# Weight conversions of the next expert issued within the first expert's second product

## The chip, the cores and the metric

The kernel runs on one core of a Trainium2 chip. The metric is the device time of one execution in microseconds (us). TensorE (PE) multiplies matrices, ScalarE (ACT) and VectorE (DVE) work element by element, GpSimd (POOL) issues the gathers and scatters by index and does some element work, and SyncE (SP) issues the other transfers. The engines run at the same time, each through its own queue of instructions in a fixed order, and wait for each other by semaphores.

## The reference

Attention in which a query sees only the keys of its own cluster, and behind it a mixture of 16 experts (4 groups of 4), where each token goes to one expert:

```python
scores = scale * np.matmul(q, k.transpose(0, 1, 3, 2))
scores = np.where(mask, scores, -1000000000.0)
...
attn = attn / (np.sum(attn, axis=-1, keepdims=True) + 1e-09)
return np.matmul(attn, v).astype(np.float32)
...
        h = np.maximum(xg[mask_e] @ w1[g, e], 0.0)
        ye = h @ w2[g, e]
        combined = g_w[mask_g][mask_e] * e_w[mask_e]
        tok_idx = np.where(mask_g)[0][mask_e]
        out[tok_idx] = combined[:, None] * ye
```

There are 4 x 768 = 3072 tokens of 512 numbers; `w1` of an expert is 512 x 1024, `w2` is 1024 x 512, all float32. The change touches the experts alone.

## The kernel before

**Two parts.** To about 404 us the kernel does the attention and the routing; from there to the end it works through the experts. Tokens are sorted to experts on the chip, each expert has a number of places for tokens (288 for the largest, then fewer), and what doesn't fit is done by a loop at the end, which isn't entered with these inputs.

**Precision.** Each float32 matrix is split into a high and a low float16 part, and a product is made of three matmuls (high x high, high x low, low x high). So each piece of weights has to be converted: `split_chunk` (L948) has ACT write the high part (L952, tile `wh0a` and so on) and DVE the low one (L955, `wl0a`) from a landed piece of float32 weights (`st`). From the 13th piece on POOL does every second high part. Activations are split in the same way: `hh` (ACT, L1172) and `hl` (DVE, L1173) from the bank `psh` of the first product, `yh` (ACT, L1195) and `yl` (DVE, L1196) from the bank `psy` of the second. There are three banks for `psh`, two for `psy` and three for `psm`, which transposes and the last step use.

**The stream of weights.** Weights come in pieces (chunks) of 512 KB: 128 partitions x 1024 float32, four for `w1` and four for `w2` of an expert. `stream` (L1093) is a generator: each step has SP issue the load of a chunk (L945) six ahead of the one that it then converts. A load waits until one of the six buffers for `st` is free, which is when DVE has made the low part of an earlier chunk. Before the loads of an expert's first chunk SP reads the number of that expert into a register (L992, an instruction `TENSOR_LOAD` of the tile `ei`, with two small ones behind it). Tiles with `0` are of `w1`, with `1` of `w2`; `a` and `b` alternate from expert to expert, so the first chunks of the stream go into `wh0a`, then into `wh0b` and `wh1b`.

**The first expert and the group of 128.** The expert with most tokens goes first (`part_a`); its weights were converted during the attention. It has 288 tokens: `up` (L1157) makes eight groups of twelve matmuls (L1170), then `down` (L1176) makes four tiles of 24 matmuls (L1192), each in a bank `psy` that is emptied by `yh` and `yl`. Here the result has features on the partitions; `settle` (L1218) later transposes it back by matmuls with `back` (L1228, three tiles of eight matmuls into `psm`), ACT scales it (`y`, L1234), and POOL scatters it to the output (L1235).

Behind it comes a group of 128 tokens of the same expert (those over 288), the pass with `k = -1` of `ranks` (L1398). Its tokens were transposed at the step `SLT = 13` of the first expert's loop. In this pass PE does eight groups of twelve matmuls of 128 columns (tile `xT`, `wh`, `wl` into `psh`); its second product (L1206) is spread over the next pass, as is each expert's. Then come the expert of rank 0 (288 tokens, weights `wh0a` and `wl0a`), rank 1, and so on.

**What sets the order.** The order of each engine's queue is that of the Python calls, save where `issue_after` puts an instruction behind a named one. In pass -1, at each `i` of the eight groups that is in `FILL` (all eight), one step of `stream` is taken, with its instructions put behind the last gather issued (`self.got`) and behind the eviction `yev[1 + i // 2]` of the first expert. At `i = 5` the tokens of the next expert are transposed (L1142, L1140) and copied to `xT` (L1143): thirds one and three by ACT, the middle one by DVE. At `i = 6` `settle` is called. In the later passes a step of the stream is put behind the last `hl` (`self.ev`). Gathers of tokens (L1127) run on POOL: six in a row for the group of 128 and the first two experts' tokens before the first expert's second product is done, three more while the tokens are transposed.

Of the kernel before, what the change touches and what calls it, by code (L numbers as in the profile page):

```python
# [15 lines left out]
AF = mybir.ActivationFunctionType  # L16
# [870 lines left out]
class Experts:  # L887
# [6 lines left out]
    short = ()  # L894
    AHEAD = 6
    SLT = 13
    FILL, SETTLE, TOK = (0, 1, 2, 3, 4, 5, 6, 7), 2, 5
    HI = (0, 1, 0, 1, 0, 1, 0, 1)
    LEAD = 12
# [257 lines left out]
    def up(self, xT, M, W, h):  # L1157
        nc, R = self.nc, self.R
        KD, FC = R.KD, self.F // P
        w1h, w1l = W  # L1160
        hh = self.xp.tile([P, FC, M], F16, name="hh")
        hl = self.xp.tile([P, FC, M], F16, name="hl")
        h += [hh, hl]
        for f in range(FC):
            fs = slice(f * P, (f + 1) * P)
            ph = next(self.ps_h).tile([P, 512], F32, name="psh")
            i = 0
            for k in range(KD):
                for w, a in ((w1h, 0), (w1h, 1), (w1l, 0)):
                    self.mm = nc.tensor.matmul(out=ph[:, 0:M], lhsT=w[:, k, fs], rhs=xT[:, a, k], start=i == 0, stop=i == 3 * KD - 1)  # L1170
                    i += 1
            nc.scalar.activation(out=hh[:, f], in_=ph[:, 0:M], func=AF.Relu)  # L1172
            self.ev = nc.vector.scalar_tensor_tensor(out=hl[:, f], in0=ph[:, 0:M], scalar=0.0, in1=hh[:, f], op0=ALU.max, op1=ALU.subtract)  # L1173
            yield

# [222 lines left out]
    def ranks(self, bg):  # L1398

        E, sizes = self.R.E, self.sizes  # L1400
        xT, xgs, down = self.xTB, self.xg0, iter(())
        for k in range(-1, E - 1):
            M = self.caps[k] if k >= 0 else P
            if 0 <= k < E - 2:
                xgs = self.gathers(k + 1)
            h = []
            up = self.up(xT, M, self.weights_of(k, 0) if k >= 0 else self.WA[0:2], h)
            for i in range(8):
                while k >= 0 and self.ready < 4 * k + (4 if i >= 4 else 2) or k > 0 and self.ready2 < 4 * k - 4 + (4 if i >= 4 or not self.feature_major(self.caps[k - 1]) else 2):
                    next(self.fill)  # L1410
                next(up, None)
                next(down, None)
                if i == (self.SETTLE if k >= 0 else 6):
                    if k == E - 2:
                        self.tc.keep_in_program_order(self.nc.gpsimd.drain())
                    self.settle()
                if i in self.FILL:
                    with ExitStack() as order:
                        for op in (self.got, self.yev[min(1 + i // 2, 3)]) if k < 0 else (self.ev,):
                            order.enter_context(self.tc.issue_after(op.ins))  # L1420
                        next(self.fill, None)
                if i == self.TOK and k + 1 < E - 1:
                    with self.tc.issue_after(self.mm.ins):
                        nT = self.tokens(xgs, self.caps[k + 1], k < 0)
                if k > 1 and i == 3:
                    with self.tc.issue_after(self.ev.ins):
                        next(bg, None)
            for s in (up, down):
                for _ in s:
                    pass  # L1430
            xT = nT
            if k >= 0:
                cols = [(self.gates[0:m, t, k:k + 1], self.ids[0:m, t, k:k + 1]) for t, m in enumerate(sizes[k])]
                down = self.down(h, M, self.weights_of(k, 1), [g for g, _ in cols], [i for _, i in cols])
            else:
                down = self.down(h, M, self.W2, [self.gB], [self.idB])
        for _ in self.fill:
            pass
        for i, _ in enumerate(down):
            if i == 0:  # L1440
                self.settle()
        self.settle()
        for _ in bg:
            pass
# [102 lines left out]
def tile_cluster_attention_moe(ctx, tc, qT, kT, vr, cen, wr, w1, w2, out):  # L1547
    nc = tc.nc
# [20 lines left out]
    X = Experts(ctx, tc, R, w1, w2, out, stage, wa)  # L1569
# [15 lines left out]
    for i, _ in enumerate(ga):  # L1585
        with tc.issue_after(X.mm.ins):
            if i == X.SLT:
                X.xTB = X.tokens([X.xB], P)

    def late():  # L1590
        yield from X.lists()
        yield from fix.detect()
        fix.finish()
        yield
# [32 lines left out]
```

## Time and profile before

| | |
|---|---|
| median of 3 runs | 744.16 us |
| lowest and highest | 742.54 and 745.04 us |
| the profiled execution, its own time | 743.51 us |
| its span in the trace | 741.8 us |
| PE busy in the span | 717.7 us (97%) |
| DVE busy | 603.6 us (81%) |
| POOL busy | 495.0 us (67%) |
| ACT busy | 481.0 us (65%) |

Times in the trace count from the start of the span. The profile names engine, source line and operation, with the tile that is written and the tiles that are read; an entry `[1.71 <-DVE yl L1196]` behind an instruction says that its engine was idle for 1.71 us before it and what ended that. An instruction's duration overlaps that of its successor by the depth of the pipeline, so the distance from one start to the next is what an instruction costs in a row of such.

### The profile page before, as it was taken

How to read it: one execution, taken by the hardware profiler on the slowest of the kernel's cores; microseconds unless marked ns; L12 is line 12 of the kernel's file. 1: busy time of each engine (PE TensorE's matmuls, PEld its weight loads, DVE VectorE, ACT ScalarE, POOL GpSimd, SP SyncE). 2: the span in 40 equal slices, each digit the busy share in tenths (PEclk: the TensorE clock that was granted, in tenths of full speed). 3: DMA queues.
4: the chain of work that ended last, by engine and by line, in shares of the span. 5: the costliest groups of instructions: out<-in, count | busy, mean ns of one | idle time of the engine just before them, and what ended most of it. 6: DMA issues, size and time to landing. Idle time of an engine off the chain costs nothing.

```text
span 741.8 us, 26652 instructions
## 1 busy us (share of the span) xinstructions
PE 717.7 (97%) x11068; PEld 618.8 (83%) x11068; DVE 603.6 (81%) x1221; ACT 481.0 (65%) x941; POOL 495.0 (67%) x493
## 2 busy tenths in 40 slices
PE   5999999999999999999999989999999999999996
PEld 3688888888888888888888777888789999999996
DVE  7798978799788997989876476767779889999971
ACT  4669877788768887677877176444545455565642
POOL 8899787787787877878787325454744668545632
PEclk9999999999999999999999999999999999999998
DMA  8745734535245351340520696877777688888921
GB/s 259 183 108 163 218 97 117 163 99 152 58 129 176 93 155 45 77 131 2 172 88 24 228 312 216 271 225 223 236 244 234 221 276 270 291 274 267 295 75 35
DMA packets 78616, 128.03 MB, mean 173 GB/s; under 512 B 7667, under 2 KB 45427, under 8 KB 78488
## 3 DMA queue, kind: packets, MB, share of 16 engines
q1 hardware_dynamic: 73404, 112.63, 50.2%
q0 software_dynamic: 4928, 13.59, 5.1%
q8 instruction: 88, 1.44, 0.8%
q14 instruction: 40, 0.33, 0.1%
q10 hardware_dynamic: 156, 0.03, 0.0%
HBM read 93.41 MB, written 13.65 MB: 144 GB/s over the span
## 4 chain that ended last, share of the span: by engine, by line
PE 64%; DVE 17%; issue 6%; ACT 5%; DMA 4%; POOL 2%; POOLq 0%; SPq 0%; DVEq 0%; ACTq 0%
PE psh L1170 14%; PE psy L1192 11%; PE pso L386 6%; PE pso L387 6%; PE psf L360 6%; PE psf L361 6%; DVE mpart L321 5%; PE psc L318 5%; PE psy L1206 3%; DMA B<-parts 2%; PE psm L699 1%; DVE parts L213 1%; ACT p L365 1%; DMA st<-w 1%; PE psm L1228 1%
## 5 line engine op out<-in xcount | busy, mean ns | idle before, releaser
L367 POOL TENSOR_TENSOR pl<-p 128x512 f16<-128x512 f32 x278 | 285.1, 1041 | 72.5 <-ACT p L365 67.9
L321 DVE TENSOR_REDUCE mpart<-psc 128x1 f32<-128x512 f32 (+1 forms) x282 | 190.5, 684 | 29.0 <-PE psc L318 28.5
L365 ACT ACTIVATE p<-psf 128x512 f32<-128x512 f32 x288 | 170.1, 597 | 49.6 <-PE psf L361 44.3
L386 PE MATMUL pso<-V,p 128*128 128x65 f16 x1152 | 160.3, 193 | 0.0
L387 PE MATMUL pso<-V,pl 128*128 128x64 f16 x1152 | 160.0, 193 | 0.0
L386 PE MATMUL pso<-V,pl 128*128 128x65 f16 x1152 | 159.5, 193 | 0.0
L387 PE MATMUL pso<-V,p 128*128 128x64 f16 x1152 | 159.3, 193 | 0.0
L360 PE MATMUL psf<-A 82*128 82x384 f16 (+2 forms) x576 | 144.1, 275 | 1.0 <-ACT p L365 0.9
L361 PE MATMUL psf<-B 128*128 128x384 f16 (+2 forms) x576 | 144.2, 275 | 0.0
L387 PEld LDWEIGHTS <-p 128*128 128x128 bf16 x1152 | 112.3, 97 | 22.1 <-issue 0.2
L386 PEld LDWEIGHTS <-p 128*128 128x128 bf16 x1152 | 113.2, 98 | 9.2 <-issue 1.1
L386 PEld LDWEIGHTS <-pl 128*128 128x128 f16 x1152 | 112.7, 98 | 0.2
L387 PEld LDWEIGHTS <-pl 128*128 128x128 f16 x1152 | 111.5, 97 | 0.1
L318 PE MATMUL psc<-A 80*128 80x512 f16 (+1 forms) x376 | 108.5, 332 | 0.8 <-DVE mpart L321 0.4
L1173 DVE SCALAR_TENSOR_TENSOR hl<-psh,hh 128x160 f16<-128x160 f32 (+14 forms) x136 | 49.7, 368 | 45.6 <-ACT hh L1172 36.6
L1172 ACT ACTIVATE hh<-psh 128x160 f16<-128x160 f32 (+14 forms) x136 | 45.6, 345 | 58.0 <-PE psh L1170 54.9
L1235 POOL DMA_INDIRECT out_dram<-y,ri x33 | 42.0, 1272 | 50.7 <-ACT y L1234 45.3
L1170 PE MATMUL psh<-xT,wh0a 128*128 128x288 f16 (+7 forms) x512 | 74.6, 255 | 0.0
L1127 POOL DMA_INDIRECT xg<-xbuf,ri x25 | 38.6, 1543 | 41.7 <-PE psm L1142 27.9
L361 PEld LDWEIGHTS <-B 128*128 128x128 f16 x576 | 56.9, 99 | 10.6 <-issue 2.0
L1170 PE MATMUL psh<-xT,wh0b 128*128 128x272 f16 (+6 forms) x448 | 64.7, 253 | 0.0
L360 PEld LDWEIGHTS <-A 82*128 82x128 f16 x576 | 56.2, 99 | 10.0 <-issue 1.8
(370 smaller groups left out, 1792.7 us busy)
## 6 DMA issues: line engine op xcount, KB each, us to landing
st<-w SPq DMA_DIRECT2D x128, 512.0 KB
B<-parts SPq DMA_DIRECT2D x64, 192.0 KB
kx<-kT SPq DMA_DIRECT2D x16, 384.0 KB
qx<-qT SPq DMA_DIRECT2D x16, 384.0 KB
vx<-vr SPq DMA_DIRECT2D x16, 384.0 KB
A<-parts SPq DMA_DIRECT2D x32, 192.0 KB
xbuf<-xs SPq DMA_DIRECT2D x4, 1536.0 KB
A<-mk SPq DMA_DIRECT2D x56, 24.0 KB
```

Source lines behind the costliest of these rows:

```text
L318: last["mm"] = nc.tensor.matmul(out=pc[:, off:off + k1 - k0], lhsT=QA[h % 8][0:80, c * P:(c + 1) * P], rhs=KA[h % 8][0:80, k0:k1], start=T ...
L321: nc.vector.tensor_reduce(out=(mp[:, 0, 0:1], mp[:, :, 1], mp[:, 1, 0:1])[i], in_=pc.rearrange("p (a x) -> p a x", a=n), axis=AX.X, op=ALU ...
L360: nc.tensor.matmul(out=o, lhsT=KA[h % 8][0:82, ks], rhs=QA[h % 8][0:82, q0:q1], start=True, stop=False)
L361: nc.tensor.matmul(out=o, lhsT=KBs[h][:, ks], rhs=QBs[h][:, q0:q1], start=False, stop=True)
L365: cfg["exp"] = nc.scalar.activation(out=p32, in_=pf, func=AF.Exp, scale=QK / (SQ * SQ))
L367: lo = (nc.vector if u in (EARLY if h < 2 else DVE_LO[h % 8] if h < NH - 2 else DVE_END) else nc.gpsimd).tensor_tensor(out=pl, in0=p32, in ...
L386: nc.tensor.matmul(out=O[:, col:col + 65], lhsT=p[:, bs], rhs=vh, start=c == 0 and q == 0 and i == 0, stop=False, skip_group_check=True)
L387: nc.tensor.matmul(out=O[:, col:col + 64], lhsT=p[:, bs], rhs=vl, start=False, stop=c == NCH - 1 and i == 1, skip_group_check=True)
L1170: self.mm = nc.tensor.matmul(out=ph[:, 0:M], lhsT=w[:, k, fs], rhs=xT[:, a, k], start=i == 0, stop=i == 3 * KD - 1)
L1172: nc.scalar.activation(out=hh[:, f], in_=ph[:, 0:M], func=AF.Relu)
L1173: self.ev = nc.vector.scalar_tensor_tensor(out=hl[:, f], in0=ph[:, 0:M], scalar=0.0, in1=hh[:, f], op0=ALU.max, op1=ALU.subtract)
L1192: self.mm = nc.tensor.matmul(out=py[:, 0:M], lhsT=w[:, f, d * P:(d + 1) * P], rhs=a[:, f], start=i == 0, stop=i == len(prods) - 1)
```

## The change

Steps of the stream are now also taken in the loop over the first expert's own steps: at steps 10, 12, 14 and 15 of 16 (`SOON`), put behind the last `hl`, the last gather and the last `yh`. In pass -1 only `i` = 1, 3, 5 and 7 take a step (`FILL0`), put behind the last gather and the last `hh` (`self.act`, new). The later passes are as before. Line numbers of the changed kernel are higher by one from L897 on, and by up to six at the end.

```diff
     SLT = 13
+    SOON, FILL0 = (10, 12, 14, 15), (1, 3, 5, 7)
     FILL, SETTLE, TOK = (0, 1, 2, 3, 4, 5, 6, 7), 2, 5
...
-            nc.scalar.activation(out=hh[:, f], in_=ph[:, 0:M], func=AF.Relu)
+            self.act = nc.scalar.activation(out=hh[:, f], in_=ph[:, 0:M], func=AF.Relu)
...
-                if i in self.FILL:
+                if i in (self.FILL if k >= 0 else self.FILL0):
                     with ExitStack() as order:
-                        for op in (self.got, self.yev[min(1 + i // 2, 3)]) if k < 0 else (self.ev,):
+                        for op in (self.got, self.act) if k < 0 else (self.ev,):
                             order.enter_context(self.tc.issue_after(op.ins))
                         next(self.fill, None)
...
             if i == X.SLT:
                 X.xTB = X.tokens([X.xB], P)
+        if i in X.SOON:
+            with ExitStack() as order:
+                for op in (X.ev, X.got) + tuple(X.yev[-1:]):
+                    order.enter_context(tc.issue_after(op.ins))
+                next(X.fill)
```

ACT's queue in the kernel before, from the first expert's first eviction `yh` to the middle of the group of 128 (`hh` of 128 x 128 belongs to that group, `wh0a`, `wh0b` and `wh1b` are converted chunks):

```order
L1195 ACTIVATE yh<-psy 128x288 x2
L952 ACTIVATE wh0a<-st 128x2x512 x2
L1195 ACTIVATE yh<-psy 128x288
L952 ACTIVATE wh0a<-st 128x2x512 x2
L1195 ACTIVATE yh<-psy 128x288
L952 ACTIVATE wh0b<-st 128x2x512
L1172 ACTIVATE hh<-psh 128x128
L952 ACTIVATE wh0b<-st 128x2x512
L1172 ACTIVATE hh<-psh 128x128 x2
L952 ACTIVATE wh1b<-st 128x4x256 x2
L1172 ACTIVATE hh<-psh 128x128 x2
L952 ACTIVATE wh0b<-st 128x2x512
```

The same stretch of ACT's queue in the changed kernel:

```order
L1196 ACTIVATE yh<-psy 128x288
L953 ACTIVATE wh0a<-st 128x2x512
L1196 ACTIVATE yh<-psy 128x288
...
L953 ACTIVATE wh0a<-st 128x2x512 x2
L1196 ACTIVATE yh<-psy 128x288
L1173 ACTIVATE hh<-psh 128x128 x2
L953 ACTIVATE wh0b<-st 128x2x512
...
L1173 ACTIVATE hh<-psh 128x128
L953 ACTIVATE wh1b<-st 128x4x256
L1144 COPY xT<-psm 128x8x128
```

The first two conversions stand each behind an eviction of their own, and in the group of 128 all four conversions into `wh0b` (left out: three more pairs of one `hh` and one `wh0b`) stand ahead of the first into `wh1b`.

DVE's queue in the kernel before, from the last `yl` of the first expert to the copy of the next tokens:

```order
L1196 SCALAR_TENSOR_TENSOR yl<-psy,yh 128x288
L955 SCALAR_TENSOR_TENSOR wl0b<-st,wh0b 128x2x512
L1173 SCALAR_TENSOR_TENSOR hl<-psh,hh 128x128 x3
L955 SCALAR_TENSOR_TENSOR wl0b<-st,wh0b 128x2x512
L955 SCALAR_TENSOR_TENSOR wl1b<-st,wh1b 128x4x256
L1173 SCALAR_TENSOR_TENSOR hl<-psh,hh 128x128 x2
L955 SCALAR_TENSOR_TENSOR wl1b<-st,wh1b 128x4x256
L1173 SCALAR_TENSOR_TENSOR hl<-psh,hh 128x128
L1143 COPY xT<-psm 128x8x128
```

And in the changed kernel:

```order
L1197 SCALAR_TENSOR_TENSOR yl<-psy,yh 128x288
L1174 SCALAR_TENSOR_TENSOR hl<-psh,hh 128x128 x2
L956 SCALAR_TENSOR_TENSOR wl0b<-st,wh0b 128x2x512
L1174 SCALAR_TENSOR_TENSOR hl<-psh,hh 128x128 x2
L956 SCALAR_TENSOR_TENSOR wl0b<-st,wh0b 128x2x512
L1174 SCALAR_TENSOR_TENSOR hl<-psh,hh 128x128 x2
L1144 COPY xT<-psm 128x8x128
L956 SCALAR_TENSOR_TENSOR wl1b<-st,wh1b 128x4x256
```

Two low parts instead of four stand ahead of the copy, and they stand between pairs of `hl`.

SP's queue in the kernel before, where the sixth load of the stream has been issued (`TENSOR_LOAD` of `ei` reads an expert's number; five more follow at once, and only then the seventh load):

```order
L945 ISA
L945 DMA st_11820<-w1 128x2x512
L992 TENSOR_LOAD ei_11487
L992 ISA x2
L992 TENSOR_LOAD ei_11487
```

And in the changed kernel at the same place:

```order
L946 ISA
L946 DMA st_11724<-w1 128x2x512
L946 ISA
L946 DMA st_11755<-w2 128x4x256
L993 TENSOR_LOAD ei_11487
```

The seventh load, which waits for the first free buffer, stands ahead of the register loads. On PE three matmuls of L1206 stand one group of L1170 later, and the first tile of `settle` takes the bank that DVE's copy frees, the second and third those that ACT's copies free. POOL's queue is unchanged.

## Rows read from the trace of the kernel before

**Rows 1.** Waits of PE, 404:742 (waited for: us in total, times, longest us).

```profile
PE psy L1192 <- DVE yl L1196: 2.1, 2, 1.7
PE psh L1170 <- issue: 0.9, 2, 0.5
```

**Rows 2.** Waits of PE, 444.5:742, all of them.

```profile
PE psy L1192 <- DVE yl L1196: 0.4, 1, 0.4
```

**Rows 3.** Timeline of PE, 421:445 (start us, us, instruction xcount [idle before <-releaser]).

```profile
421.77 1.14 PE L1192 MATMUL psy<-hl,wh1a 128*128 128x288 f16 x8
...
427.57 1.14 PE L1192 MATMUL psy<-hh,wh1a 128*128 128x288 f16 x8 [1.71 <-DVE yl L1196]
...
435.90 0.38 PE L1206 MATMUL psy<-wh1a,hh 128*128 128x512 f16 x1
436.12 0.38 PE L1206 MATMUL psy<-wl1a,hh 128*128 128x512 f16 x1
436.96 0.27 PE L1170 MATMUL psh<-xT,wh 128*128 128x128 f16 x2 [0.46 <-DVE hl L1173]
...
438.97 1.06 PE L1142 MATMUL psm<-ident,xg 128*128 128x128 f16 x16
...
440.07 0.27 PE L1170 MATMUL psh<-xT,wh 128*128 128x128 f16 x2
...
441.19 0.22 PE L1228 MATMUL psm<-back,yh 128*128 128x128 f16 x1 [0.30 <-ACT xT L1143]
...
442.53 0.28 PE L1170 MATMUL psh<-xT,wh 128*128 128x128 f16 x2
...
444.42 0.41 PE L1170 MATMUL psh<-xT,wh0a 128*128 128x288 f16 x2
```

**Rows 4.** Timeline of ACT, 419:458.

```profile
426.62 0.71 ACT L1195 ACTIVATE yh<-psy 128x288 f16<-128x288 f32 x2 [6.19 <-PE psy L1192]
...
434.10 0.41 ACT L1195 ACTIVATE yh<-psy 128x288 f16<-128x288 f32 x1 [1.08 <-PE psy L1192]
...
438.98 1.09 ACT L952 ACTIVATE wh0b<-st 128x1024 f16<-128x1024 f32 x1
439.93 0.31 ACT L1172 ACTIVATE hh<-psh 128x128 f16<-128x128 f32 x1
440.09 1.06 ACT L1143 COPY xT<-psm 128x1024 f16<-128x1024 f16 x1
...
444.13 0.28 ACT L1172 ACTIVATE hh<-psh 128x128 f16<-128x128 f32 x1 [1.75 <-PE psm L1228]
...
453.97 1.06 ACT L952 ACTIVATE wh1a<-st 128x1024 f16<-128x1024 f32 x1 [2.38 <-DMA st<-w]
```

**Rows 5.** Timeline of DVE, 419:446.

```profile
427.06 0.82 DVE L1196 SCALAR_TENSOR_TENSOR yl<-psy,yh 128x288 f16<-128x288 f32 x2 [6.15 <-ACT yh L1195]
...
432.12 2.35 DVE L955 SCALAR_TENSOR_TENSOR wl0a<-st,wh0a 128x1024 f16<-128x1024 f32 x2
...
441.23 0.68 DVE L1143 COPY xT<-psm 128x1024 f16<-128x1024 f16 x1
```

**Rows 6.** Timeline of POOL, 414:446: the last gather of each of the two rows.

```profile
424.08 0.95 POOL L1127 DMA_INDIRECT xg<-xbuf,ri  x1 [0.30 <-issue]
...
442.26 0.97 POOL L1127 DMA_INDIRECT xg<-xbuf,ri  x1 [0.30 <-issue]
```

**Rows 7.** SP's register loads (L992), 420.5:426.6, 434.5:440, 440:446 (ns min/median/max, starts us).

```profile
L992 SPq TENSOR_LOAD <-ei x6: 3/262/278, 420.9 to 425.0; - x6
...
L992 SPq TENSOR_LOAD <-ei x2: 264/276/289, 434.9 to 437.2; - x2
...
L992 SPq TENSOR_LOAD <-ei x5: 3/267/396, 441.6 to 444.2; - x5
```

**Rows 8.** DMA queues, 416:437.2 (packets, MB, share of 16 engines): SP's queue.

```profile
q1 hardware_dynamic: 2944, 4.70, 65.4%
```

**Rows 9.** Stretch 416:450 (us, busy of PE PEld DVE ACT POOL, PEclk, DMA share, GB/s).

```profile
416.00:450.00 34.00, 30.62 (x328) 24.44 (x327) 17.22 (x32) 19.50 (x35) 12.37 (x13) 1.00 0.86 297
```

## Prediction

> **What bounds the kernel now.** I read the waits of TensorE (PE) first, over the experts' stretch from 404 us on. They are short: the largest is PE waiting for an eviction in the first expert's second product, then 0.9 us put down to "issue" [rows 1]. From 444.5 us to the end PE waits once, for 0.4 us [rows 2]. So PE is the bound, and behind 444.5 us nothing can be won or hidden: whatever time the first matmul of expert 0's first product (444.42 us [rows 3]) moves by, the end moves by.
>
> The order of instructions shows that the change touches nothing after the first steps of that product. The question is therefore only when that matmul starts. Between 420 and 444.4 us PE stands still five times: 1.71 us before 427.57, 0.46 before 436.96, 0.30 before 441.19 [rows 3], and the two "issue" gaps, 0.9 together [rows 1]. These 3.4 us are all that can be gained, 0.46% of the time.
>
> Next I read ScalarE (ACT) and VectorE (DVE) there [rows 4, 5]. From 434.10 us ACT runs without a pause (the rows left out between 434.10 and 440.09 note no idle time): an eviction, conversions, evictions, the copy of the next tokens (440.09 for 1.06, to 441.15). PE's transposing back of the first expert's result starts 0.04 us behind that copy, at 441.19 [rows 3]. In this group of 128 ACT, not PE, sets the pace, and the change reorders ACT's queue there.
>
> **The change, part by part.** I call the chunks of weights c0, c1, ... in the order of the stream.
>
> *First product's evictions and loads.* Nothing is added or removed: same twelve conversions, same loads, same matmuls. The first six loads and the six gathers stand where they stood.
>
> *Second product of the first expert.* Before, ACT has two yh, c0, c1, yh, c2, c3, yh; now yh, c0, yh, c1, yh, c2, c3, yh. Four conversions stand ahead of the fourth yh in both, so "begins inside" is a move by one place. The 1.71 us stall is PE's third tile waiting for the first tile's bank, freed by yl at 427.06 + 0.46 [rows 3, 5] behind the first yh at 426.62 [rows 4]. Both stand first in both orders: the stall stays if yh starts when it did. c0 now goes ahead of the second yh, which costs PE nothing: yh 426.62, c0 to 427.98, yh to 428.3, on DVE wl of c0 to 429.2 and yl to 429.7, while PE needs that bank only after 24 matmuls and eight transposes, behind 430.9. Third and fourth tile go as before; the fourth yh is again at 434.10 [rows 4].
>
> *Why the first yh is so late.* Its eight last matmuls run from 421.77 for 1.14 us [rows 3], so its bank is full at 422.9, and ACT has been idle for 6.19 us when it starts at 426.62 [rows 4]: 3.7 us unexplained by the order. In that time POOL issues six gathers in a row, the last ending at 425.03 [rows 6], and SyncE (SP) six loads of registers, from 420.9 to 425.0 [rows 7]. The second bad place is alike: three gathers, the last ending at 443.23 [rows 6], five register loads between 441.6 and 444.2 [rows 7], and an hh at 444.13 on an ACT that was idle for 1.75 us [rows 4]; PE's own "issue" gaps fall there too. What is late is the signal. Which of the two causes it no row tells. The gathers stay; the change moves the six register loads behind the load of c6, that is behind 429 us. The bounds of this term are thus 0 (stall stays) and -1.71 us (it goes). I take 0, since long runs of gathers stand at both places and stay; the other end is a rival.
> The Trainium skill, page "Advanced Engine Details and Errata", section "Miscellaneous Facts", has 50 to 100 ns for a sequencer's reading of a semaphore. By that alone yh starts at 423.0 and the stall is nothing, which leads to the first rival; the rows above say 3.7 us in this stretch, and I follow them.
>
> *Group of 128.* Behind the fourth yh ACT had c4, hh, c5, hh, hh, c6, c7, hh, hh, c8, hh, copy, cast. Now it has hh, hh, c4, hh, c8, hh, c5, hh, c9, hh, c6, copy, cast. Five conversions before the copy in both; but c8 is now the second of them, and was the fifth. c8 is the ninth load, 9 x 0.524 = 4.72 MB into SP's queue; 4.70 MB had started by 437.2 us [rows 8], and ACT took c8 at 438.98 without waiting [rows 4]. It landed between those; its last packets still have to arrive after they start, so I take 438.4, near the upper end. It can't be issued before DVE's third wl0a, 433.3 us [rows 5], which the change doesn't move.
>
> Sum for ACT, with 0.95 us from a conversion's start to the next start (438.98 to 439.93) and some 0.2 for an hh (439.93 to 440.09 [rows 4], and a little more where it waits for PE): hh and hh behind PE's first two groups, 435.5; c4 to 436.6; hh; c8 waits until 438.4, ends 439.45; hh 439.65; c5 440.6; hh 440.8; c9 441.7; hh 441.9; c6 442.85; copy 443.8; cast 444.1.
> DVE behind it, 1.2 us for a wl (2.35 for two [rows 5]): hl 2 behind wl of c4, 438.15; hl 3 at 439.95; wl of c5 to 441.85; hl 4 at 442.1; then its own copy of the middle third of the tokens, to 442.85.
> PE, with 0.67 us for a group of twelve (three from 436.96 to 438.97), 1.10 for the 40 transposes and copies (to 440.07), 0.45 for a tile of settling (1.34 for three) [rows 3]: the fourth group no longer waits for DVE's wl (the 0.46 goes) and ends at 436.6; three matmuls of 0.22 [rows 3]; the fifth group to 437.9; the sixth needs hl 2: 438.2 to 438.9; transposes to 440.0; the seventh needs hl 3: to 440.65; the eighth's first two matmuls need hl 4, 442.1; settling's first tile, now on the bank of DVE's copy, 442.9 to 443.35; three matmuls; second tile behind ACT's copy, 443.85 to 444.3; third to 444.75; the seven left, 445.15. **Expert 0 starts at 445.15 instead of 444.42: +0.7 us.** With c8 landed at 437.2 it would be -0.5, at 438.98 +1.3.
>
> *Later loads.* wl of c6 and c7 come after the tokens' copy, so the loads of c12 and c13 go out some 4 to 7 us later than before. The first chunk behind c11 is converted at 453.97, after ACT waited 2.38 us for its load [rows 4], and PE doesn't feel that wait [rows 2]: its product has banks of 1.4 us each in hand (eight matmuls of 288 take 0.98 [rows 3]). A longer wait there is hidden by the same; if that cover were gone, the cost would be one chunk's time, 0.524 MB at the 297 GB/s of 416 to 450 us [rows 9], 1.76 us. I take 0.
>
> TensorE's granted clock is 1.00, its upper level (2.4 GHz), from 416 to 450 us [rows 9], so no term comes from it.
>
> The profiled execution took 743.51 us (span 741.8 and 1.7 around it), 0.65 below the median of the runs, 744.16. So 743.51 + 0.7 = 744.2 for a like execution, and **744.9** set against the median.
>
> **Rivals.**
> 1. *The register loads were the cause.* Gone from among the gathers, the first yh starts at 423 and PE runs on: the group of 128 starts 1.71 us sooner. But ACT then meets c8 sooner and waits longer: loads c6 and c7 go out earlier, yet SP's queue was already busy, so c8 lands at most about 0.9 us earlier, 437.5; from there the same chain gives 444.3, -0.1: 744.1. For: at both bad places the register loads stand in bunches, and the two single ones between them, at 434.9 and 437.2 [rows 7], go with no late signal. Against: gathers are at both places too.
> 2. *Slower: the late signals hit the new chain.* In the old order PE hardly depended on ACT between 440.9 and 444.1; now the path runs from ACT's hh through DVE's hl and copy to settling. If signals given after 440.8 arrive only at 444.1 as they did (hh at 444.13 [rows 4]), hl 4 is at 444.4, DVE's copy at 445.25, settling and the last matmuls 1.95 more: 447.2, +2.8 us: 747.0. It decides from about 1.5 us of delay on. For: the gathers before 443.23 stay in place. Against: only two register loads are left there, and a delay must fall on these very signals.
> 3. *Faster: c8 is in time.* The stall of 1.71 goes and c8 has landed by 435, so ACT never waits: copy to 440.5, settling from 439.5 to 441.4, expert 0 at 441.8, -2.6 us: 741.5. Against: 4.72 MB had not started by 437.2 in a queue with no long pauses; no row shows how they would come 2 us sooner.
> 4. *It does nothing*, since its main move is one place: 744.2.
>
> **How the numbers follow.** Forecast 45%, rival 1 27%, rival 4 2%: together 74% within 0.3%, which is 2.2 us and about what a measurement of this kernel tells from no change. Rival 2 18%, slower by more than that; rival 3 8%, faster. The likeliest is 744.9. The range leaves out rival 3 and the upper part of rival 2: from 742.6 (the early end of the landing, 0.5 below rival 1, and a us for the spread of the runs, 742.5 to 745.0) to 747.2.
>
> **What would show it.** In the new trace: the idle of ACT before the first yh, 6.2 us again if the gathers delay signals, about 2.5 if the register loads did; a wait of ACT for a load ahead of the second conversion in the group of 128, 1.5 us; no wait of PE before the fourth group; a wait of 1 to 1.5 us before the eighth, and shorter ones in settling; expert 0's first matmul 0.7 us later against the span's start; from there on the same rows. The prediction is wrong if PE waits behind 446 us, if c8 isn't waited for, or if the signals' delay has moved to where the new order depends on it.

## The result and the profile after

| | before | after |
|---|---|---|
| median of 20 runs each, taken side by side | 741.40 us | 746.39 us |
| lowest and highest | 739.35 and 745.04 us | 742.47 and 749.40 us |
| after : before | | 1.0063, 95% interval 1.0051 to 1.0075 |
| the profiled execution, its own time | 743.51 us | 747.89 us |
| its span | 741.8 us | 746.2 us |

The changed kernel is slower by 0.63%, 4.7 us by the ratio. 746.39 us lies inside the range of the prediction, near its upper end. But "slower by more than 0.3%" had been given a chance of 0.18, and the likeliest value, +0.7 us on the kernel before, was too small by a factor of more than six. The three runs of the kernel before that the prediction started from (median 744.16) lie above most of its later ones; that is probably part of the explanation.

In what follows, c0, c1, ... are the chunks of weights as in the prediction, and lines of the changed kernel are one higher. The largest waits of PE in the changed kernel from 404 us on (engine, line and what it waited for: us in total, times, longest us), the answer to [rows 1]:

```profile
PE psh L1171 <- DVE hl L1174: 3.0, 2, 1.8
PE psy L1193 <- DVE yl L1197: 1.7, 2, 1.3
PE psm L1229 <- DVE xT L1144: 0.5, 1, 0.5
```

The 1.7 us of `yl` are no longer the stall of [rows 1]; they lie behind 520 us, in two pieces. The 3.0 us are new. PE's timeline shows where they are (start us, us, instruction, xcount, [idle before <-releaser]); it answers [rows 3]:

```profile
427.20 1.14 PE L1193 MATMUL psy<-hh,wh1a 128*128 128x288 f16 x8
...
438.47 1.06 PE L1143 MATMUL psm<-ident,xg 128*128 128x128 f16 x16
...
441.47 0.27 PE L1171 MATMUL psh<-xT,wh 128*128 128x128 f16 x2 [1.75 <-DVE hl L1174]
...
443.55 0.27 PE L1171 MATMUL psh<-xT,wh 128*128 128x128 f16 x2 [1.25 <-DVE hl L1174]
444.35 0.26 PE L1229 MATMUL psm<-back,yh 128*128 128x128 f16 x1 [0.52 <-DVE xT L1144]
...
445.47 0.31 PE L1229 MATMUL psm<-back,yh 128*128 128x128 f16 x1
445.58 0.31 PE L1229 MATMUL psm<-back,yl 128*128 128x128 f16 x1
...
447.74 0.41 PE L1171 MATMUL psh<-xT,wh0a 128*128 128x288 f16 x2
```

The third tile of the second product (427.20) starts without a wait. The seventh group of the 128 tokens waits 1.75 us, the eighth 1.25, settling 0.52. And settling's matmuls then stand 0.107 us apart (445.47, 445.58), where [rows 3] had 24 of them in 1.34 us (441.19 to 442.53). ACT's timeline of the changed kernel has the source, and answers [rows 4]:

```profile
424.46 0.41 ACT L1196 ACTIVATE yh<-psy 128x288 f16<-128x288 f32 x1 [2.53 <-PE psy L1193]
...
436.19 0.27 ACT L1173 ACTIVATE hh<-psh 128x128 f16<-128x128 f32 x1
439.87 1.06 ACT L953 ACTIVATE wh0b<-st 128x1024 f16<-128x1024 f32 x1 [3.41 <-DMA st<-w]
440.83 0.26 ACT L1173 ACTIVATE hh<-psh 128x128 f16<-128x128 f32 x1
...
444.15 1.02 ACT L1144 COPY xT<-psm 128x1024 f16<-128x1024 f16 x1
```

ACT stands 3.41 us in front of c8's conversion, waiting for its load; behind it stand the evictions of the fourth to sixth group and the copy of the next tokens. The first `yh`, late in [rows 4], starts as soon as its bank is full. The stretches (us, busy of PE, PEld, DVE, ACT, POOL with counts, granted clock, DMA share, GB/s), as in [rows 9]:

```profile
421.32:433.53 12.21, 12.21 (x106) 9.84 (x104) 6.57 (x9) 5.42 (x8) 4.94 (x6) 1.00 1.01 359
433.53:439.00 5.47, 5.36 (x87) 4.84 (x85) 3.05 (x6) 2.08 (x5) 0.00 (x0) 1.00 1.02 351
439.00:444.10 5.10, 1.82 (x32) 1.50 (x30) 2.32 (x5) 4.23 (x7) 2.77 (x3) 1.00 0.67 202
444.10:447.50 3.40, 3.15 (x31) 3.15 (x31) 1.85 (x5) 2.87 (x7) 1.02 (x1) 0.50 0.79 217
```

From 439.0 to 444.1 us PE is busy for 1.82 of 5.10 us; then its granted clock is 0.50 (1.2 GHz) for 3.4 us, just when it has work again. Up to 439 us the DMA engines are busy without a gap (share 1.01 and 1.02), and c8's load, issued at 433.3 us, lands at 439.85 us. By the trace's record of landings the first of its sixteen landing signals comes at 437.4 and the last at 439.85; ACT's conversion starts at 439.87. That the loads and gathers around it hold it up fits the full engines, but no run here shows it by itself.

### The profile page after: what moved, and what is told of

It reads as the page before. It is cut to its first block, busy times and chain, and to the rows that moved or that the text cites. A ratio compares the mean times of both kernels' runs of the same rounds, so it can differ in the third digit from the quotient of the medians.

```text
span 746.2 us, 26654 instructions
## 1 busy us (share of the span) xinstructions
PE 719.6 (96%) x11068; PEld 621.2 (83%) x11068; DVE 599.9 (80%) x1221; ACT 480.8 (64%) x941; POOL 493.9 (66%) x493
## 4 chain that ended last, share of the span: by engine, by line
PE 62%; DVE 18%; issue 7%; DMA 5%; ACT 4%; POOL 3%; POOLq 0%; SPq 0%; ACTq 0%; DVEq 0%
PE psh L1171 14%; PE psy L1193 10%; PE pso L386 6%; DVE mpart L321 6%; PE pso L387 6%; PE psf L360 5%; PE psf L361 5%; PE psc L318 5%; PE psy L1207 3%; DMA st<-w 2%; DVE parts L213 2%; PE psm L699 1%; PE psm L1229 1%; DMA vx<-vr 1%; ACT p L365 1%
## 5 line engine op out<-in xcount | busy, mean ns | idle before, releaser
L1128 POOL DMA_INDIRECT xg<-xbuf,ri x25 | 38.6, 1543 | 40.0 <-PE psm L1143 26.4
```

## The experiments

**A measure for one trace.** Behind expert 0's first matmul PE's longest wait is 0.4 us in the first trace of the kernel before [rows 2] and 1.26 us in that of the changed kernel. So each trace is reduced to starts on PE, counted from the first matmul of the first expert's second product: the first group of the 128 tokens, the transposes of the next tokens, settling, and expert 0's first matmul. Each is the start of the corresponding row of PE's timeline less the start of that first one (419.81 before, 421.32 after). "Rest" is the span less expert 0's start. "c8" is the last landing signal of c8's load, counted in the same way. The kernels are explained below.

| trace | group of 128 | transposes | settling | expert 0 | rest | c8 |
|---|---|---|---|---|---|---|
| before | 14.08 | 19.16 | 21.38 | 24.61 | 297.4 | 18.57 |
| before again (b_rep) | 12.20 | 17.28 | 19.66 | 21.67 | 298.3 | 17.46 |
| after | 12.21 | 17.15 | 23.03 | 26.42 | 298.5 | 18.53 |
| after again (a_rep) | 13.09 | 18.03 | 22.85 | 26.13 | 297.8 | 18.35 |
| after, third time (a_rep2) | 12.21 | 17.15 | 22.84 | 26.20 | 297.2 | 18.35 |
| b_regs | 13.04 | 18.12 | 20.34 | 23.66 | 298.2 | 18.09 |
| a_early | 13.92 | 18.86 | 22.83 | 26.32 | 296.8 | 18.34 |
| b_g2 | 12.20 | 17.28 | 19.74 | 21.76 | 297.9 | 17.53 |
| a_order | 13.79 | 18.73 | 20.57 | 22.67 | 300.0 | 18.18 |
| a_dense | 12.21 | 17.81 | 20.55 | 22.56 | 297.6 | 18.35 |
| a_busy | 12.21 | 17.15 | 21.88 | 24.32 | 301.6 | 17.39 |

The traces are of two kinds: the group of 128 starts at 12.20 or 12.21 us, or 0.8 to 1.9 us later. The second kind has the late signals of the prediction. b_regs, a_early, a_order and a_rep were taken one after the other and all have them; of the later ones in the table none has. The kernel before took 744.36 us (median of 35) beside the first four, and 741.98 (17) and 742.53 us (23) beside the others, 741.40 (20) beside the first runs of the changed kernel. That fits late signals that cost the kernel before some 2 to 3 us outside the profiled execution too, though no trace shows those executions.

**Do the register loads hold up the signals? (b_regs)** The kernel before, each register load pinned behind the weight load ahead of it (`self.ld`, the load issued last):

```diff
-                    er[r] = self.load_reg(self.ei[0:1, r:r + 1], self.R.E - 1)
+                    with self.tc.issue_after(self.ld.ins):
+                        er[r] = self.load_reg(self.ei[0:1, r:r + 1], self.R.E - 1)
```

> The kernel before, with SP's register loads for ranks 2 and up put behind the weight loads that precede them in the stream, so that none stands among the gathers. Nothing else moves. Theory R (the bunch of register loads beside the gathers holds back the signals): ACT's first yh starts within 0.5 us of its bank being full (its idle time 2.5 instead of 6.2 us), PE's stall of 1.71 us is gone, the two issue gaps (0.9 us) and the 1.75 us of ACT before its late hh too; from the first matmul of the second product to expert 0's first matmul 22.0 to 23.0 us instead of 24.6; time 1.6 to 2.6 us below the kernel before. Theory G (the rows of gathers alone do it): all of this as before, 24.6 us, time within 0.5 us.

743.08 us (12 runs) beside 744.36, ratio 0.9988 (0.9968 to 1.0007). SP's register loads in this stretch of its trace (ns min/median/max, first and last start us), and ACT's first `yh` (`remote`: the trace doesn't tell what ended the wait):

```profile
L992 SPq TENSOR_LOAD <-ei x2: 273/278/283, 418.4 to 437.5; - x2
```

```profile
425.10 0.41 ACT L1196 ACTIVATE yh<-psy 128x288 f16<-128x288 f32 x1 [5.16 <-remote]
```

Two register loads, none between 419 and 437 us, and the first `yh` is late all the same: its bank was full at 422.4 us, it starts at 425.10. Theory R falls.

**The other way round (a_early).** The changed kernel with six register loads back ahead of the seventh weight load:

```diff
+                if n == 6:
+                    with self.tc.issue_after(self.ld.ins):
+                        for x in range(2, 8):
+                            er[x] = self.load_reg(self.ei[0:1, x:x + 1], self.R.E - 1)
```

> The changed kernel, with six register loads put back where the kernel before has them, ahead of the stream's seventh load. The order on ACT, DVE, PE and POOL is that of the changed kernel. Theory R: the first yh is late again by 3 to 4 us and PE stalls some 1.7 us in the second product; the wait for c8's load gets shorter by what was lost ahead of it, since the load hardly moves; time 0 to 1.7 us above the changed kernel. Theory G: as the changed kernel, no stall in the second product, within 0.5 us of it.

745.49 us beside 744.36, ratio 1.0022 (1.0003 to 1.0040); the changed kernel itself, run beside it, 745.71. In the trace the stall is there (1.55 us), as theory R says; but a_rep beside it, without these loads, has late signals too. What the run shows is something else: the group of 128 starts 1.7 us later than in the first trace of the changed kernel, and expert 0 at 26.32 against 26.42. The loss ahead of the group is swallowed.

**The changed kernel again (a_rep, a_rep2).**

> The changed kernel once more, for its spread. Its profile had, beside the 1.8 us in the group of 128, a fall of the granted clock at 24 to 33 us (about 1.5 us) and a wait of PE of 1.26 us at 705 us. If these belong to the program, both recur and they explain that the medians lie 4.7 us apart and not 1.8. If they belong to the single execution, one or both are missing, and the medians' remaining 3 us has another cause. Time 4 to 5.5 us above the kernel before.

745.71 us (12 runs), ratio 1.0027 (1.0008 to 1.0045) to the 744.36 beside it: 1.35 us more, not the 4 to 5.5 expected. The wait at 705 us isn't there (one of 0.4 us is), a fall of the clock at 24 us is, the waits and the fall at 444 us are.

> The changed kernel a third time, as the partner of the others. With signals in time: 26.2 to 26.6 us to expert 0's first matmul, waits of PE of about 1.75, 1.25 and 0.5 us, clock at 0.50 for 3.4 us from 444 us on, 4 to 5 us above the kernel before in the median, since the kernel before then has no stall and this one's load lands no earlier. With signals late: 26.1 to 26.3 us and 1 to 2 us above.

747.58 us (7 runs), ratio 1.0065 (1.0040 to 1.0089) to 742.53. The fall at 24 us is missing, and neither early fall nor late wait is needed for the 4.8 us: with signals in time the traces of the two kernels differ by 26.2 or 26.4 less 21.7 up to expert 0. By estimate 0.9 to 1.1 us of that are c8's landing: both chains run through its conversion, and it lands sooner in b_rep (17.46) than in the two (18.35 and 18.53). c8's conversion starts at 439.53 here, at 438.82 in a_rep and 439.13 in a_early:

```profile
438.82 1.06 ACT L953 ACTIVATE wh0b<-st 128x1024 f16<-128x1024 f32 x1 [2.36 <-DMA st<-w]
```

```profile
439.53 1.06 ACT L953 ACTIVATE wh0b<-st 128x1024 f16<-128x1024 f32 x1 [3.23 <-DMA st<-w]
```

From the second product's start that is 18.37 (a_rep), 18.37 (a_rep2), 18.36 (a_early) and 18.55 us (the first trace), whether signals were late or not, and always 0.02 us behind c8's landing. The load sets it, and ACT's wait is whatever is left. The landing itself isn't fixed, though: in the table it lies between 17.39 us (a_busy, with c8 in the same place) and 18.57.

**The kernel before again (b_rep).**

> The kernel before once more. So far a trace either has the late signals (ACT idle 5 to 6 us ahead of the first yh) or not, and traces taken one after the other on the chip agree: late in the first trace of the kernel before and in b_regs, a_early, a_order, a_rep; in time in the trace of the changed kernel and in soon_act, b_g2 and ord5, with and without six gathers, early and late register loads. Theory S (it belongs to the time at which the chip is used, not to an order of instructions): if the kernels run beside it have the first yh in time, so has this one, and then it takes 21.5 to 22.5 us from the first matmul of the second product to expert 0's first matmul instead of 24.6. Theory G (the gathers of this order): late again whatever the others show, 23.7 to 24.6 us.

One run, 743.60 us. Theory S holds: the kernels beside it have signals in time, so has this one. Its waits of PE from 404 us on, and ACT's first evictions:

```profile
PE psy L1192 <- DVE yl L1196: 0.6, 2, 0.4
PE psh L1170 <- DVE hl L1173: 0.5, 1, 0.5
PE psm L1228 <- ACT xT L1143: 0.5, 1, 0.5
```

```profile
425.06 0.41 ACT L1195 ACTIVATE yh<-psy 128x288 f16<-128x288 f32 x1 [2.53 <-PE psy L1192]
...
439.41 1.06 ACT L952 ACTIVATE wh0b<-st 128x1024 f16<-128x1024 f32 x1
440.38 0.26 ACT L1172 ACTIVATE hh<-psh 128x128 f16<-128x128 f32 x1
440.54 1.00 ACT L1143 COPY xT<-psm 128x1024 f16<-128x1024 f16 x1
```

Same program as in [rows 1 to 5]: no stall of 1.71 us, no "issue" gap, no late `hh`. Its c8 is converted at 439.41, 17.48 us after the start, without a noted wait: in the old order the load has just landed (17.46) when its turn comes.

**Fewer gathers (b_g2).** The kernel before with `bufs=2` in place of `bufs=5` for the gathered tokens `xg`.

> The kernel before with two buffers for gathered tokens instead of five: two gathers instead of six run beside the first expert's second product, the others wait for PE's transposes (431 us and later). The order on ACT, DVE, PE and SP stays. Theory G (the row of six gathers holds back the signals): the first yh starts within 0.5 us of its bank being full, the 0.7 to 1.7 us stall in the second product is gone, 22.5 to 23.5 us to expert 0's first matmul, time 1 to 2 us below the kernel before. If something else holds the signals back: a stall of 0.7 to 1.7 us as in five of the six traces so far, time within 0.5 us of the kernel before.

743.10 us (12 runs), ratio 1.0013 (0.9993 to 1.0033) to 741.98. Signals in time, 21.76 us. But b_rep has that with six gathers, so the run tells nothing of theory G. It was made at a time without late signals; what makes them late stays open.

**c8 back in its place (a_order).** ACT's first twelve conversions pinned in stream order:

```diff
         if eng == 0:
-            nc.scalar.activation(out=h, in_=st, func=AF.Copy, scale=WS)
+            with self.tc.issue_after(self.cv.ins) if self.cv is not None and self.ncv < 12 else ExitStack():
+                self.cv = nc.scalar.activation(out=h, in_=st, func=AF.Copy, scale=WS)
+            self.ncv += 1
```

> The changed kernel, with ACT's first twelve conversions pinned in the order of the stream, so that c8 and c9 come behind c7; in the group of 128 only c4, c5 and c6 are left ahead of the copy of the next tokens. Theory W (the loss is ACT's wait for c8's load, with PE's clock falling in the waits that it makes): no wait of ACT for a load in the group of 128, no wait of PE over 0.6 us there, granted clock 1.00 from 433 to 450 us; from the first matmul of the second product to expert 0's first matmul 21.5 to 22.5 us instead of 26.4; time 4 to 5 us below the changed kernel, so 0 to 3 us below the kernel before. Rival L (the loss is in later loads, which go out late behind c6 and c7): the wait of ACT goes, but the time stays 2 us or more above the kernel before.

742.91 us (12 runs) beside 745.71 for the changed kernel; to the kernel before 0.9988 (0.9968 to 1.0008). The wait is gone, the clock stays at 1.00, and expert 0 starts at 22.67 us although the signals are late, 3.5 us sooner than in a_rep. The rest is 1.5 to 3 us longer, though. Waits of PE from 444 us on:

```profile
PE psy L1196 <- DVE yl L1200: 1.2, 3, 0.4
PE psh L1174 <- DVE hl L1177: 0.8, 2, 0.5
```

With three conversions ahead of the copy instead of five, buffers come free later, and so do loads; ACT waits for them (for one of `wh1a` 5.7 us; the longest such wait in the kernel before is 3.8), evictions stand behind it, and PE loses 2.0 us. So W's wait and L's price both show here, but neither time came: W expected 4 to 5 us below the changed kernel (it is 2.8), L 2 us or more above the kernel before (it is 1.45 below).

**The thinning alone taken back (a_dense).** The changed kernel with `FILL0 = (0, 1, 2, 3)` in place of `(1, 3, 5, 7)`.

> The changed kernel with its four conversions of the group of 128 at places 0 to 3 instead of every second one. The scheduler then leaves c8 behind c7, so ACT has c4, c5, c6, c7, c8, one behind each hh, ahead of the copy; the conversions inside the second product stay. Theory W (the loss is c8's place, which the thinning makes, and not the early conversions): no wait of ACT for a load ahead of the copy, clock 1.00, 21.5 to 23 us to expert 0's first matmul, time within 1 us of the kernel before with signals in time. If the early conversions lose something themselves, the time stays 2 us or more above the kernel before.

742.60 us (12 runs) beside 742.53, ratio 0.9996 (0.9977 to 1.0015). ACT there (no other row between the first and the copy notes idle time):

```profile
433.81 0.28 ACT L1173 ACTIVATE hh<-psh 128x128 f16<-128x128 f32 x1 [0.26 <-PE psh L1171]
433.98 1.05 ACT L953 ACTIVATE wh0b<-st 128x1024 f16<-128x1024 f32 x1
...
437.75 1.06 ACT L953 ACTIVATE wh1b<-st 128x1024 f16<-128x1024 f32 x1 [0.34 <-DMA st<-w]
438.72 0.26 ACT L1173 ACTIVATE hh<-psh 128x128 f16<-128x128 f32 x1
439.11 1.06 ACT L953 ACTIVATE wh0b<-st 128x1024 f16<-128x1024 f32 x1
...
440.23 1.00 ACT L1144 COPY xT<-psm 128x1024 f16<-128x1024 f16 x1
```

c4 to c8 in order, c8 at 18.4 us from the start with its load just landed, the copy at 440.23. So the conversions inside the second product cost and win nothing that this comparison can tell; the loss is the thinning's, through c8's place. In the trace settling and expert 0 do start 0.89 us later than in b_rep: ACT begins c4 behind the first `hh`, 13.25 us from the start and not 12.71, and then waits 0.34 us for c7. The medians don't show it.

**The clock (a_busy).** The changed kernel with idle matmuls in the waits (the helper's core; it is called behind the transposes with 28 and ahead of the eighth group with 18). Two more edits of the run aren't shown here: the last two groups of the 128 stand behind the idle matmuls, and in expert 0's pass the stream's steps at `i` = 2 and 3 are put behind ACT's `y` too:

```diff
+    def idle(self, py, op, n):
+        with self.tc.issue_after(op.ins):
+            for _ in range(n):
+                self.dm = self.nc.tensor.matmul(out=py[:, 0:P], lhsT=self.R.ident, rhs=self.R.ident, start=True, stop=True)
```

> The changed kernel with idle work for PE in the two longest waits: 28 matmuls of 128 columns behind the transposes of the next tokens and 18 ahead of the eighth group, into a bank of psy that nothing reads (six matmuls of the group's second product thereby move behind expert 0's first ones, about 0.65 us of them past its first matmul). ACT and DVE keep the changed kernel's order up to settling, the wait for c8's load stays. Theory C (1.7 us of the loss is the clock that falls to 0.50 behind the waits): clock 1.00 through 433 to 450 us, matmuls of settling again 0.055 us apart instead of 0.107, 23.5 to 25 us to expert 0's first matmul, time 1 to 2 us below the changed kernel. If the clock falls all the same or the time stays, the clock isn't worth a term.

745.76 us (11 runs) beside 747.58 for the changed kernel. PE's rows, ACT's conversion of c8, the stretch, and PE's largest wait from 404 us on:

```profile
435.44 1.72 PE L1402 MATMUL psy<-ident 128*128 128x128 f16 x28
...
437.67 1.17 PE L1402 MATMUL psy<-ident 128*128 128x128 f16 x18
439.07 0.22 PE L1229 MATMUL psm<-back,yh 128*128 128x128 f16 x1 [0.24 <-DVE xT L1144]
```

```profile
434.60 1.06 ACT L953 ACTIVATE wh0b<-st 128x1024 f16<-128x1024 f32 x1 [2.27 <-DMA st<-w]
```

```profile
433.00:442.00 9.00, 7.82 (x135) 7.48 (x135) 4.82 (x11) 7.40 (x14) 3.82 (x4) 1.00 0.81 264
```

```profile
PE psy L1193 <- DVE yl L1197: 3.3, 4, 1.7
```

The clock stays at 1.00, and expert 0 starts at 24.32; with the 0.65 us of moved matmuls added, 24.97, 1.2 us sooner than in a_rep2. But most of that isn't the clock's: c8 is converted 17.41 us after the start here and 18.37 in a_rep2, 0.96 us sooner, and settling starts sooner by as much (21.88 and 22.84). From settling to expert 0 it takes 2.44 us against 3.36; with the moved matmuls added, the filled waits have won 0.27. By its medians the kernel is 1.8 us faster, though the two ratios to the kernel before (1.0050, 1.0029 to 1.0071, and 1.0065) have overlapping intervals, and 3.3 us of waits turn up behind expert 0's start that a_rep2 doesn't have (0.4). Why these are there wasn't followed up; the pin behind `y` may be a reason. So the run shows that the clock stays up where PE's waits are filled, and doesn't price its fall. The price comes from the rows: from settling to expert 0 the first trace of the changed kernel has 34 matmuls (24, and ten of the eighth group) in 3.39 us. At the rate of [rows 3] (24 in 1.34) they take 1.9, so the half clock costs some 1.5 us there.

**Three that can't be set against the others.** The thinning without the early conversions (fill0: the `SOON` block never taken):

> The other half alone: the thinning (every second place of the group of 128, behind the last hh) without the conversions inside the second product. c4 and c5 float into that product; c0, c1, c2 stand in the group, c3 behind settling's evictions. Theory W has no c8 ahead of the copy here, so no wait for a load there and settling as in the changed kernel without the wait, 22 to 23 us to expert 0's first matmul; but PE then waits for the low part of c3 inside expert 0's first product, 1 to 3 us, and the later loads go out later: time 1 to 5 us above the kernel before.

794.50 us (6 runs), ratio 1.0702. The expectation was of the wrong size. Up to expert 0 it takes 27.74 us, not 22 to 23: c4's conversion has moved ahead of the second `yh`, ACT stands 8.18 us for its load, and PE 4.20 us for the eviction behind it. And without the four early steps the stream is four conversions behind in every later pass, and PE waits all through (ten waits with 23.1 us in all for ACT's evictions alone). The two halves of the change belong together: only both keep eight conversions ahead of expert 0.

```profile
434.32 1.06 ACT L953 ACTIVATE wh0b<-st 128x1024 f16<-128x1024 f32 x1 [8.18 <-DMA st<-w]
```

```profile
PE psy L1193 <- ACT hh L1173: 23.1, 10, 4.7
PE psy L1193 <- DVE yl L1197: 8.2, 7, 4.2
```

The early conversions without the thinning (soon_act: `if i in self.FILL` for all passes):

> The changed kernel without its thinning: in the group of 128 all eight places take a conversion again (put behind the last hh), while four are still issued inside the first expert's second product. So ACT has c4 to c9 one behind each hh, in the order of the stream, six ahead of the copy. Theory W (the loss is c8's place in ACT's queue, and the clock that falls in the waits): no wait of ACT for a load ahead of the copy, granted clock 1.00 from 433 to 450 us; from the first matmul of the second product to expert 0's first matmul 22.5 to 23.5 us instead of 26.3; time 2.5 to 4 us below the changed kernel. Rival (six conversions ahead of the copy hold settling up as much as c8's wait did): the copy ends 2 us later against the group's start than in the kernel before, 24.5 to 26 us, time as the changed kernel's.

784.96 us (6 runs). Here the stream runs four steps too far ahead: c12 is written into `wh0a` before expert 0's later groups have read c0 to c3 there, and so on in every pass, so later groups are computed with another expert's weights, and PE waits for each new conversion. Up to expert 0's first matmul the trace can be read: 23.96 us, a little over the 22.5 to 23.5 expected, settling at 21.54. With six conversions ahead of the copy settling starts 1.0 us later than with five in a_dense (20.55). And conversions in stream order with five places (ord5: a_order with `FILL0 = (1, 2, 3, 4, 5)`):

> The changed kernel with conversions pinned in stream order and five places in the group of 128 (1 to 5), so c4 to c8 stand ahead of the copy as in the kernel before, c8 last of them. Theory W: no wait for a load there, clock 1.00, 22 to 23 us to expert 0's first matmul. The pinned order with three conversions ahead of the copy won 1.9 us up to that matmul and gave it back by waits of PE behind it (its loads went out later: ACT waited 3.7 us for one of wh0b, PE 2.0 us in all). With five, the buffers come free as early as before: PE's waits behind 448 us stay under 0.6 us, and the time is 1 to 3 us below the kernel before. If the gain is given back here too, the later loads weren't the cause and the time is within 1 us of the kernel before.

747.02 us (6 runs), 22.97 us to expert 0's first matmul, as expected, and no wait of ACT for a load ahead of the copy. One step too far: c12 replaces a part of `wh0a` that expert 0's last groups still had to read. The waits behind it (3.5 us for ACT's evictions) belong to that, so the question about later loads isn't answered by it.

## Why the prediction was right and wrong

**Right: where, and by what.** That the bound is PE, that only expert 0's start matters and the rest stays: the rest is 297.2 to 298.5 us in all traces of both kernels. That c8, put second in the group, makes ACT wait for its load: so it does. The landing was estimated at 438.4, 18.59 us after the second product's start; four traces with c8 in this place have the conversion at 18.36 to 18.55, a_busy at 17.41. The chain behind it was sized well too: settling was to start at 442.9, 23.09 us from the start, and starts at 22.83 to 23.03. That no PE wait is left before the fourth group is right as well. The largest wait, 1.75 us before the seventh group, it did not have: with the signals late it let PE come there at 440.0 us, 20.2 from the start, where the first trace, with signals in time, has PE there at some 18.3.

**Luck: that the result lies in the range.** The upper part of the range was drawn for rival 2, which did not occur, and the range was set around 744.16 us. Set around the 741.40 of the larger measurement it would end at 744.4, 2 us below the result.

**Wrong: that no term comes from the clock.** The sum gave 2.25 us from settling to expert 0; the trace has 3.39, and b_rep 2.01. The difference is the clock at 0.50 from 444.1 to 447.5. The prediction had read the clock in the kernel before [rows 9] and carried it over, although it forecast itself that PE would wait at three places close together. The Trainium skill, page "TensorE: Matmul & The Clock Gate", section "HAM oscillation — how this bites in real kernels", says that waits for DMA can drop PE's clock so that the next work starts at half rate; the trace agrees, though PE's waits here are for DVE, with 1.82 us of work in the 5.10 us ahead and 0.50 behind. Of 4.75 us between b_rep and the first trace of the changed kernel, 3.50 lie between transposes and settling (5.88 against 2.38, the waits) and 1.38 between settling and expert 0 (the clock); ahead of these it gains 0.13. a_busy shows that the clock stays up with the waits filled. Its 1.2 us can't be taken for the price, since 0.96 of them are c8's landing.

**Wrong: the base.** The stall of 1.71 us, the late `hh` and the "issue" gaps were taken for parts of the kernel before, which the changed kernel might lose or keep. They are parts of an execution: the same program has them in one trace (24.61) and not in another (21.67). The chain through c8 hides them, the old order doesn't. So the change costs 26.1 to 26.3 less 24.6, some 1.6 us, where signals are late (some 2.6 against b_regs' 23.66), and 4.5 to 4.75 us where they are in time, 0.9 to 1.1 of it, by estimate, by c8's landing; the medians say 1.0027 and 1.0063 or 1.0065. The prediction's own +0.7 us was made on the first base; with the 1.1 us that the clock adds to it (3.39 less 2.25) it would have been +1.8, close to the difference of the two first traces (26.42 less 24.61). What it missed was to set the same doubt ("which of the two causes no row tells") against the kernel before: its own 25.34 us for the new order (24.61 and 0.73), which hang on c8's landing, are +3.7 us on b_rep's 21.67, and +4.8 with the clock.

**The rivals.** The first (register loads) had its effect in the first trace of the changed kernel and the wrong cause: b_regs has no such loads and late signals. Its time was wrong by two more steps: it let c8 land at 437.5, 17.7 us from the start, where the trace has 18.53 (a_busy's 17.39 shows that this can happen), and it kept the late signals in the kernel that it compared with. The second gave 747.0 us, close to the result, for a reason that didn't occur: no signal is late on the new chain. That is luck. The third and fourth are out. *Later loads* at nothing was right for the changed kernel; a_order shows the price when it does come, 2.0 us of PE's waits.

**The sentence on reading a semaphore** (Trainium skill, "Advanced Engine Details and Errata", "Miscellaneous Facts") was set aside for the row. Where signals are in time the trace is near the page's figure: the last eight matmuls ahead of the first `yh` end at 424.42 (423.28 and 1.14 us; such ends are modelled), and it starts at 424.46.

**A count.** The prediction speaks of 40 transposes; its rows have 24 (16 and eight). The 1.10 us that it takes for them is that of the rows.

## What to carry to other kernels

An order pin on one engine leaves the other engines' part of the same step free: here DVE's half of c8's conversion was pinned and ACT's was not, and as soon as the row of conversions was thinned, the scheduler filled the place with one whose data weren't there. For every instruction that moves up, ask when its data land, counted from a fixed point of the busy engine, and plan for the late end (here 17.4 to 18.6 us, in traces of the same kernel too). Price PE's waits that stand close together with a stretch at half clock behind them. And a stall in a single trace that no instruction explains may belong to that execution: work the sum out for both kernels with it and without it.

## What the runs showed of the hardware

Signals between engines can be late by 2.6 to 3.7 us at a time (a first `yh` 5.16 to 6.19 us after the instruction before it, where 2.53 is usual), in runs of several kernels one after the other, and then for none. Neither SP's register loads (b_regs is late without them) nor the order of instructions (the same program is late in a_rep and in time in a_rep2) makes the difference. Beside the late traces the kernel before takes 2 to 3 us more in the median (744.36 against 741.40 to 742.53), the changed kernel nothing that can be told apart (745.71 us; 746.39 and 747.58 otherwise). The cause wasn't found. The late traces also hold fewer records of semaphore updates (10,294 to 10,354 in the five of the table, 10,790 to 10,801 in the other six), so the recording itself may have a part in it; no run here tells.

ACT's conversion of c8 starts 0.02 us behind the last of the sixteen landing signals of its load, and these spread over 16.07 to 18.53 us from the second product's start in the first trace of the changed kernel and over 16.07 to 17.39 in a_busy; in a_rep fifteen are there by 17.32 and the last at 18.35. What holds the last ones back wasn't followed up.
